# Feed-forward buffers over a whole chunk, the two linear polynomial parts once per chunk, and the first chunk in halves

## The chip, the cores and the metric

The kernel runs on one core of one Trainium2 chip. The metric is the device time of one execution in microseconds (us). Before the change six runs took 249.60 to 254.32 us, with a median of 250.72. The core has five engines that work through their own instruction lists in order and wait for each other by semaphores: TensorE (PE, matmuls), VectorE (DVE), ScalarE (ACT), GpSimd (POOL) and SyncE (SP). Here POOL and SP do little more than start transfers, which the core's 16 DMA engines carry out.

## The reference

The first half is an attention with polynomial features, for 4 batches, 4 heads, 1088 tokens and head width 32. With S1 and S2 of 8 rows each, the features of a row x are the 64 products of S1 x and S2 x. The output of the first half is

```python
kv  = einsum('bhsf,bhsd->bhfd', phi(k), v)
num = einsum('bhsf,bhfd->bhsd', phi(q), kv)
den = einsum('bhsf,bhf->bhs', phi(q), sum(phi(k), over s))[..., None] + 1e-06
x   = (num / den), heads side by side: 4352 tokens x 128
```

The second half is a feed-forward layer with d_ff = 2048 and a rational function between its two matrices:

```python
h = x @ w_in
P = a[0] + a[1]*h + a[2]*h*h + a[3]*h*h*h
Q = 1.0 + abs(b[0])*abs(h) + abs(b[1])*h*h
out = (P / (Q + 1e-06)) @ w_out
```

Inputs and output are float32.

## The kernel before

**Chunks and groups.** Of each batch's 1088 tokens 1024 are two chunks of 512; the 64 left over from each of the four batches form one last chunk of 256. That makes nine chunks, n = 0 to 8. The feed-forward part of a chunk works on tiles with 128 partitions (one block of d_ff) and, along the free axis, blocks times tokens. A group is a set of d_ff blocks: chunks 1 to 7 have two groups of 8 blocks (8 x 512 = 4096 columns), chunk 0 has groups of 4, 4 and 8, the last chunk 8, 4 and 4 blocks of 256 columns. The groups are numbered through, g0 to g19.

**The polynomial.** x is scaled by the ratio of the coefficients (sig) on its way into xT, and a is scaled to match (inv), so that Q is 1 + lsc * (|h| + h*h) up to the small constant. For each group, `add_group` adds these steps: PE makes h in pieces of 1024 columns in PSUM (L572), ACT or DVE evicts each piece to hb in bfloat16 (L184, L186). DVE computes the square s = hb*hb (sq, L582), u = |hb| (ab, L585), the upper linear part t = a3*hb + a2 (hi, L603), t = t*s (cu, L607), and the lower linear part in place, hb = a1*hb + a0 (lo, L610). Two sums follow, u + s (us) and t + hb (ts). Most of them are accumulating transfers that POOL issues (L594), a few run on DVE (L592). ACT takes Ln and then Exp with scale -1 (L614, L618), which gives 1/Q in u. DVE multiplies t by u (ov, L621), and PE projects t with W_out into out_ps (pj, L629). After a chunk's last group out_ps is evicted to oT and stored by SP.

**The attention's steps** are spread between these. For each half batch of keys: transposes (tr), eviction (ev), projection (pr), eviction of a part (ea), products k_p on DVE (pd, L403); then kv. For each chunk of queries: transposes, eviction to qT, two expansions into PSUM (ex0, ex1, L499), eviction of the first to A_sb, their product q_pT on DVE (L506), numerator and denominator on PE in two parts (nd0, nd1, L519), the division in three DVE instructions (dv, L526 to L529), transposes of x (xt, L535) and the scaled eviction to xT (xe, L540 or L542).

**What sets the order.** `plan.add` only collects steps with a name, an engine and their dependencies. ORDER is a list of step numbers written out in full; `Plan.issue` emits the steps in that order, and so fixes the order on each engine. ENGINE names the steps that go to another engine than the default, HOME the PSUM pool of some steps, SKIP the filler matmuls (L746) left out. BUFS gives the number of buffers of each kind. A buffer is taken by the step that names it in `take` and freed when all steps have been emitted that name it in `give`. In the built program an instruction that takes over a buffer waits for the last readers and writers of what lay there: hb, u and t have four buffers and s two, each of one group's 4096 columns.

Of the kernel before, what the change touches and what calls it, by code (L numbers as in the profile page):

```python
# [12 lines left out]
FP = mybir.dt.float32  # L13
# [6 lines left out]
FIRST = [4, 4, 8]  # L20
LAST = [8, 4, 4]
LW = 4096
FILLS = 16

BUFS = dict(xT=3, hb=4, s=2, u=4, t=4, k_sb=2, v=1, q=2, L=1, h_ps=3, out_ps=1, w_ps=1,
            kT=1, a_t=2, k_p=2, qT=2, A_sb=1, q_pT=1, den=1, x=1, oT=1)

ENGINE = {
    "ld.S0": "ACT", "ld.S1": "ACT", "ld.a": "ACT", "ld.b": "ACT", "k00.ea": "DVE", "k01.ea": "DVE", "kr.ev": "DVE",
    "kr.ea": "DVE", "k0.s0": "DVE", "q1.ev": "DVE", "q2.ev": "DVE", "k20.ea": "DVE", "q5.xe": "DVE", "k30.ea": "DVE",  # L30
    "k31.ea": "DVE", "q7.ev": "DVE", "q8.xe": "DVE", "g1.ts": "DVE", "o0.eT": "DVE", "o1.eT": "DVE", "g7.e4": "DVE",
    "o3.eT": "DVE", "o5.eT": "DVE", "g13.e4": "DVE", "g17.us": "DVE", "g18.ts": "DVE", "o8.eT": "DVE",
}

FOUR = []
SKIP = ["f3"]

HOME = {
    "k00.T": "h_ps", "k00.ab": "h_ps", "k01.T": "h_ps", "k01.ab": "h_ps", "kv.0": "h_ps", "q0.T": "h_ps",
    "q0.xT": "h_ps", "q1.T": "h_ps", "k11.T": "h_ps", "q2.T": "h_ps", "q2.xT": "h_ps", "q3.T": "h_ps",  # L40
    "q3.xT": "h_ps", "k20.T": "h_ps", "k21.T": "h_ps", "kv.2": "h_ps", "q4.T": "h_ps", "q5.T": "h_ps",
    "q6.T": "h_ps", "q8.T": "h_ps", "q8.xT": "h_ps", "fill.1": "h_ps", "fill.4": "h_ps", "fill.6": "h_ps",
    "fill.9": "h_ps", "fill.11": "h_ps", "fill.12": "h_ps",
# [3 lines left out]
    27, 4, 26, 30, 0, 36, 1, 31, 6, 56, 20, 3, 32, 33, 37, 5, 41, 38, 39, 57, 23, 46, 29, 2, 42, 40, 58, 43, 47, 59,  # L47
    60, 44, 45, 48, 49, 50, 51, 52, 21, 53, 28, 55, 8, 61, 7, 83, 78, 79, 67, 54, 62, 63, 80, 81, 11, 34, 68, 69, 12,
    64, 65, 84, 22, 9, 66, 82, 70, 71, 72, 85, 86, 215, 216, 35, 217, 10, 87, 218, 230, 232, 231, 233, 24, 245, 16,
    220, 219, 115, 247, 116, 246, 248, 222, 224, 234, 235, 237, 223, 221, 226, 73, 74, 75, 249, 250, 238, 239, 240,  # L50
    76, 25, 251, 93, 94, 236, 77, 252, 253, 254, 227, 266, 268, 270, 88, 89, 267, 269, 256, 257, 241, 242, 95, 97,
    272, 271, 225, 14, 228, 273, 229, 243, 104, 105, 90, 258, 244, 96, 91, 92, 274, 277, 285, 98, 130, 201, 117, 99,
    100, 255, 260, 286, 13, 275, 131, 279, 259, 287, 101, 278, 289, 291, 261, 262, 288, 118, 119, 276, 200, 290, 292,
    102, 103, 120, 121, 263, 293, 294, 296, 297, 281, 306, 106, 307, 108, 122, 123, 325, 326, 280, 107, 109, 124,
    264, 298, 282, 283, 308, 309, 310, 312, 152, 295, 311, 313, 300, 265, 110, 111, 112, 327, 284, 153, 329, 314,
    315, 331, 328, 317, 318, 319, 330, 132, 332, 205, 125, 126, 301, 113, 213, 154, 334, 18, 114, 299, 155, 134, 302,
    333, 127, 128, 129, 316, 133, 346, 303, 336, 135, 338, 17, 156, 348, 321, 337, 304, 347, 349, 189, 350, 320, 190,
    365, 203, 157, 351, 322, 323, 352, 15, 136, 366, 141, 158, 137, 353, 138, 142, 335, 340, 305, 324, 367, 368, 355,
    354, 139, 339, 357, 358, 359, 369, 140, 386, 159, 341, 371, 370, 372, 342, 160, 376, 373, 374, 377, 378, 387, 19,
    143, 145, 356, 361, 360, 343, 388, 389, 344, 161, 390, 392, 391, 393, 144, 167, 362, 168, 146, 405, 395, 375,  # L60
    406, 162, 163, 164, 165, 345, 380, 381, 166, 363, 409, 147, 397, 394, 148, 149, 364, 398, 399, 407, 411, 408,
    379, 382, 150, 151, 410, 412, 414, 416, 413, 418, 169, 171, 396, 383, 178, 401, 426, 427, 428, 429, 170, 417,
    172, 179, 384, 445, 402, 430, 431, 432, 173, 446, 174, 181, 400, 433, 403, 175, 435, 404, 434, 415, 420, 437,
    180, 182, 176, 447, 177, 448, 419, 451, 421, 183, 438, 439, 449, 422, 450, 452, 454, 453, 385, 466, 467, 209,
    436, 441, 468, 469, 423, 485, 486, 424, 456, 457, 184, 185, 186, 440, 442, 470, 471, 458, 487, 472, 204, 488,
    489, 473, 443, 474, 475, 444, 477, 478, 455, 460, 191, 193, 425, 459, 187, 188, 479, 491, 490, 492, 192, 461,
    493, 194, 462, 506, 525, 526, 508, 507, 476, 494, 480, 195, 196, 463, 527, 496, 497, 464, 481, 509, 482, 498,
    495, 510, 511, 512, 513, 528, 465, 529, 483, 197, 514, 198, 515, 517, 519, 499, 500, 484, 530, 531, 214, 532,
    501, 548, 546, 533, 207, 534, 547, 516, 535, 502, 549, 553, 518, 536, 538, 520, 561, 562, 563, 537, 564, 551,
    550, 552, 521, 522, 523, 574, 540, 503, 504, 575, 576, 554, 577, 539, 555, 541, 208, 542, 566, 524, 579, 581,  # L70
    580, 568, 567, 569, 557, 558, 565, 570, 571, 505, 199, 578, 556, 559, 582, 543, 211, 206, 212, 544, 545, 210,
    560, 572, 573, 583, 584, 585, 586, 587, 588, 202,
# [40 lines left out]
def kernel(  # L113
# [27 lines left out]
    GW = GF * CW  # L141
# [14 lines left out]
    SHAPES = dict(xT=([128, CW], FP), hb=([128, GW], BF), s=([128, GW], BF), u=([128, GW], BF), t=([128, GW], BF),  # L156
# [199 lines left out]

    W_by = [big.tile([128, NF // 2, d_model], BF, name=f"w_by{i}") for i in range(4)] if FOUR else []
    by_steps = []
    if FOUR:
        ld["wf"] = load("wf", lambda key: starter(key).dma_start(  # L360
            out=new("L", "wf")[:, :NF // 2 * d_model].rearrange("p (n d) -> p n d", d=d_model),
            in_=moe_w_out.rearrange("(fo fi) d -> fi fo d", fi=128)[:, 0:NF // 2, :]), 1740, pk=1024, take=[("L", "wf")], start="SP")

        def by(i):
            o, s = W_by[i].rearrange("p n d -> p (n d)"), T["L", "wf"][:, :NF // 2 * d_model]
            if ENGINE.get(f"c.w{i}", "ACT") == "ACT":
                nc.scalar.mul(o, s, a_sb[:, i:i + 1])
            else:
                nc.vector.tensor_scalar(out=o, in0=s, scalar1=a_sb[:, i:i + 1], scalar2=None, op0=AX.mult)

        for i in range(4):
            alts = dict(ACT=280 + 0.82 * NF // 2 * d_model, DVE=150 + 0.55 * NF // 2 * d_model)
            by_steps.append(plan.add(f"c.w{i}", ENGINE.get(f"c.w{i}", "ACT"), alts[ENGINE.get(f"c.w{i}", "ACT")], lambda i=i: by(i),
                                     after=[ld["wf"], c_inv], give=[("L", "wf")], alts=alts))

# [104 lines left out]
    def add_queries(n, srcs, nt, owners, loads, kv_steps, give=()):  # L480
# [41 lines left out]
        def divide():  # L522
            nb = min(2, nt)
            nd = pair("nd")[:, :nt // nb, :nb * 132].rearrange("p b (g c) -> p b g c", c=D + 1)
            den = new("den", n)[:, :nt // nb, :nb * H]
            nc.vector.tensor_scalar(out=den, in0=nd[:, :, :, D], scalar1=1e-6, scalar2=None, op0=AX.add)  # L526
            nc.vector.reciprocal(out=den, in_=den)
            x = new("x", n)[:, :nt, :].rearrange("p (b i) (h d) -> p b (i h) d", b=nt // nb, h=H)
            nc.vector.tensor_mul(out=x, in0=nd[:, :, :, 0:D],  # L529
                                 in1=den[:, :, :, None].broadcast_to([128, nt // nb, nb * H, D]))  # L530

        def x_transposes():
            p = new(*ps(nm, "xT"))
            for i in range(nt):
                nc.tensor.transpose(p[:, i * 128:(i + 1) * 128], in_=T["x", n][:, i, :], identity=ident)  # L535

        def x_evac():
            o, i = new("xT", n)[:, :W], T[ps(nm, "xT")][:, :W]
            if ENGINE.get(nm + ".xe", "ACT") == "ACT":
                nc.scalar.mul(o, i, sig)  # L540
            else:
                nc.vector.tensor_scalar(out=o, in0=i, scalar1=sig, scalar2=None, op0=AX.mult)  # L542
# [9 lines left out]
        for i in range(nt // 2):  # L552
            nd.append(plan.add(f"{nm}.nd{i}", "PE", 520, lambda i=i: num_den(i), after=[s] + nd + kv_steps,
                               take=[("h_ps", nm, "nd")] if i == 0 else [], give=[("q_pT", n)]))
        s = plan.add(f"{nm}.dv", "DVE", 560 + 135 * nt, divide, after=nd, take=[("x", n), ("den", n)],
                     give=[("h_ps", nm, "nd"), ("den", n)])
        s = plan.add(nm + ".xt", "PE", 100 * nt + 37, x_transposes, after=[s], take=[ps(nm, "xT")], flex=[ps(nm, "xT")], give=[("x", n)])
        return add_copy(nm + ".xe", x_evac, W, ptr=1, after=[s, c_b], take=[("xT", n)], give=[ps(nm, "xT")])


    def add_group(g, G):
        W, fis, n = G["W"], G["fis"], G["n"]
        gw = W * len(fis)
        nsub = 1024 // W
# [220 lines left out]
```

## Time and profile before

The profiled execution took 249.8 us, of which its span, from the first to the last instruction, is 248.0 us. The table gives the busy time of each engine over the span, and the stages by the time since its start.

| | PE | DVE | ACT | POOL | DMA share | GB/s |
|---|---|---|---|---|---|---|
| whole span, us busy | 221.5 | 225.4 | 213.9 | 48.8 | | 182 |
| 0 to 25 us | 23.06 | 14.05 | 9.69 | 2.69 | 0.76 | 227 |
| 25 to 45 us | 19.87 | 19.80 | 16.33 | 5.55 | 0.84 | 135 |
| 45 to 95 us | 49.02 | 46.70 | 46.21 | 10.06 | 0.97 | 183 |
| 95 to 145 us | 48.80 | 49.12 | 47.94 | 9.10 | 0.99 | 190 |
| 145 to 205 us | 56.94 | 58.67 | 57.19 | 13.08 | 0.98 | 182 |
| 205 to 244 us | 23.46 | 36.63 | 36.53 | 8.36 | 0.98 | 181 |

The DMA share is the mean busy share of the 16 DMA engines. In the slices a digit is the busy share of one fortieth of the span in tenths. In a group's row stand the line, the engine, the operation, the tiles written and read, the shapes and the count; then the busy time in us and the mean of one in ns; then the time that the engine was idle just before, with what ended it. In a timeline row stand the start and the duration in us, and in brackets the idle time before it. An instruction on DVE starts a little before the one ahead of it is recorded as ended.

### The profile page before, as it was taken

The numbers are of one execution on the slowest core, as the hardware profiler recorded it, in microseconds if no ns is written. First come the engines' busy times: TensorE is split into PE (matmuls) and PEld (weight loads), VectorE is DVE, ScalarE is ACT, GpSimd is POOL, SyncE is SP. The second block draws the span as 40 slices with busy tenths as digits, with TensorE's granted clock in tenths as the row PEclk, the third lists the DMA queues.
The fourth block names the chain that finished last, engine by engine and source line by source line (L and its number), as shares of the span: only waits on it lengthen the run. The fifth ranks groups of instructions, "written<-read, shape, count | busy, mean of one in ns | idle before, by whom it ended". The sixth has DMA issues, their size and how long they took to land.

```text
span 248.0 us, 4269 instructions
## 1 busy us (share of the span) xinstructions
PE 221.5 (89%) x1779; PEld 127.2 (51%) x1789; DVE 225.4 (91%) x205; ACT 213.9 (86%) x158; POOL 48.8 (20%) x61
## 2 busy tenths in 40 slices
PE   7999999999999999999999999999998969920763
PEld 2674455654636466563557445546453627720542
DVE  0785999999989989999999999999999999998993
ACT  2336589989989798999999999899989899999991
POOL 4000422132101212112111121212121312113210
PEclk9999999999999999999999999999999999995598
DMA  5895398999998899989999999999999999999982
GB/s 150 266 323 177 69 140 178 168 220 185 186 170 183 146 189 229 231 173 167 173 196 186 180 162 188 196 169 178 200 165 183 178 198 188 182 188 185 196 162 72
DMA packets 23428, 45.11 MB, mean 182 GB/s; under 512 B 5233, under 2 KB 13553, under 8 KB 23409
## 3 DMA queue, kind: packets, MB, share of 16 engines
q0 software_dynamic: 11232, 34.87, 80.0%
q1 hardware_dynamic: 11712, 9.90, 12.8%
q8 instruction: 14, 0.23, 0.4%
q10 hardware_dynamic: 464, 0.08, 0.2%
q14 instruction: 6, 0.04, 0.0%
HBM read 8.79 MB, written 2.23 MB: 44 GB/s over the span
## 4 chain that ended last, share of the span: by engine, by line
PE 37%; DVE 28%; DMA 17%; issue 10%; ACT 6%; SPq 0%; DVEq 0%; ACTq 0%; POOLq 0%
PE h_ps L572 19%; DMA t<-hb 8%; DMA u<-s 7%; DVE s L582 6%; DVE t L621 5%; PE h_ps L499 5%; DVE t L607 5%; PE out_ps L629 4%; DVE t L603 4%; DVE u L585 3%; ACT u L618 3%; DVE hb L610 2%; PE h_ps L421 2%; DMA q<-in_q_dram 2%; PE h_ps L519 2%
## 5 line engine op out<-in xcount | busy, mean ns | idle before, releaser
L572 PE MATMUL h_ps<-xT,w_in_sb 128*128 128x512 f32 (+1 forms) x288 | 125.8, 577 | 3.2 <-ACT hb L184 2.9
L572 PEld LDWEIGHTS h_ps<-xT,w_in_sb 128*128 128x128 f32 x288 | 51.7, 190 | 55.4 <-issue 43.3
L184 ACT CAST hb<-h_ps 128x1024 bf16<-128x1024 f32 x66 | 64.6, 1018 | 8.4 <-PE h_ps L572 8.0
L614 ACT ACTIVATE L<-u,one_ap,lsc 128x4096 f32<-128x4096 bf16 (+2 forms) x20 | 65.9, 3295 | 5.4 <-DMA u<-s 5.0
L618 ACT ACTIVATE u<-L 128x4096 bf16<-128x4096 f32 (+2 forms) x20 | 62.3, 3114 | 0.2
L629 PE MATMUL out_ps<-w_out,t 128*128 128x128 bf16 x544 | 35.2, 225 | 16.0 <-DVE t L621 15.8
L594 POOL DMA_DIRECT2D u<-s x19 | 24.1, 1269 | 118.3 <-DVE u L585 54.7
L629 PEld LDWEIGHTS <-t 128*128 128x128 bf16 x544 | 32.5, 101 | 23.8 <-DVE t L621 20.7
L621 DVE TENSOR_TENSOR t<-t,u 128x4096 bf16<-128x4096 bf16 (+2 forms) x20 | 39.2, 1968 | 3.1 <-DMA t<-hb 1.7
L582 DVE TENSOR_TENSOR s<-hb 128x4096 bf16<-128x4096 bf16 (+2 forms) x20 | 39.2, 1963 | 1.5 <-ACT hb L184 1.5
L607 DVE TENSOR_TENSOR t<-t,s 128x4096 bf16<-128x4096 bf16 (+2 forms) x20 | 39.3, 1967 | 0.3
L594 POOL DMA_DIRECT2D t<-hb x18 | 21.6, 1200 | 72.2 <-ACT u L618 17.4
L610 DVE TENSOR_SCALAR hb<-hb,a_sb 128x4096 bf16<-128x4096 bf16 (+2 forms) x20 | 23.8, 1189 | 0.2
L603 DVE TENSOR_SCALAR t<-hb,a_sb 128x4096 bf16<-128x4096 bf16 (+2 forms) x20 | 23.6, 1183 | 0.0
L585 DVE TENSOR_SCALAR u<-hb 128x4096 int16<-128x4096 int16 (+2 forms) x20 | 22.3, 1115 | 0.1
L499 PE MATMUL h_ps<-qT,Srep 64*128 64x512 f32 (+1 forms) x72 | 19.5, 617 | 0.4 <-ACT hb L184 0.4
L506 DVE TENSOR_TENSOR q_pT<-A_sb,h_ps 128x1024 f32<-128x1024 f32 (+1 forms) x9 | 10.4, 1157 | 2.6 <-ACT A_sb L184 1.4
L519 PEld LDWEIGHTS h_ps<-kv,q_pT 128*64 128x64 f32 (+1 forms) x288 | 8.7, 134 | 5.1 <-issue 2.0
L519 PE MATMUL h_ps<-kv,q_pT 128*64 128x66 f32 (+1 forms) x288 | 10.1, 225 | 0.0
L184 ACT COPY A_sb<-h_ps 128x1024 f32<-128x1024 f32 (+1 forms) x9 | 8.7, 963 | 0.8 <-PE h_ps L499 0.8
L499 PEld LDWEIGHTS h_ps<-qT,Srep 64*128 64x128 f32 x72 | 5.4, 184 | 6.9 <-ACT hb L184 2.1
L184 ACT COPY kT<-h_ps 128x512 f32<-128x512 f32 x5 | 2.9, 585 | 5.4 <-PE h_ps L383 4.8
(89 smaller groups left out, 134.6 us busy)
## 6 DMA issues: line engine op xcount, KB each, us to landing
u<-s POOLq DMA_DIRECT2D x15, 1024.0 KB, 8.7
t<-hb POOLq DMA_DIRECT2D x15, 1024.0 KB, 9.3
k_sb<-in_k_dram SPq DMA_DIRECT2D x4, 512.0 KB, 4.7
q<-in_q_dram SPq DMA_DIRECT2D x8, 256.0 KB, 5.1
v<-in_v_dram SPq DMA_DIRECT2D x4, 512.0 KB, 7.9
out_dram<-oT SPq DMA_DIRECT2D x8, 256.0 KB, 6.5
w_in_sb<-in_moe_w_in_dram SPq DMA_DIRECT2D x2, 512.0 KB, 5.3
u<-s POOLq DMA_DIRECT2D x2, 512.0 KB, 7.5
```

Of the source, the lines that this page charges most:

```text
L184: nc.scalar.copy(out=out, in_=in_)
L499: nc.tensor.matmul(pair(i)[:, g, :W], lhsT=Srep[i][rows].rearrange("p g f -> p (g f)"), rhs=T["qT", n][rows, :W], start=True, stop=True)
L572: nc.tensor.matmul(p[:, i * W:(i + 1) * W], lhsT=w_in_sb[:, fi * 128:(fi + 1) * 128], rhs=T["xT", n][:, :W], start=True, stop=True)
L582: nc.vector.tensor_mul(out=new("s", g)[:, :gw], in0=h, in1=h)
L585: nc.vector.tensor_scalar(out=new("u", g)[:, :gw].bitcast(mybir.dt.int16), in0=T["hb", g][:, :gw].bitcast(mybir.dt.int16), scalar1=0x7FFF, ...
L594: nc.gpsimd.dma_start(out=d, in_=s, accum_op=AX.add, max_dma_last_dim=4096)
L603: nc.vector.tensor_scalar(out=new("t", g)[:, :gw], in0=T["hb", g][:, :gw], scalar1=a_sb[:, 3:4], scalar2=a_sb[:, 2:3], op0=AX.mult, op1=AX ...
L607: nc.vector.tensor_mul(out=T["t", g][:, :gw], in0=T["t", g][:, :gw], in1=T["s", g][:, :gw])
L614: nc.scalar.activation(out=new("L", g, l0)[:, :lw], in_=T["u", g][:, l0:l0 + lw], func=ACT.Ln, bias=one_ap, scale=lsc)
L618: nc.scalar.activation(out=T["u", g][:, l0:l0 + lw], in_=T["L", g, l0][:, :lw], func=ACT.Exp, scale=-1.0)
L621: nc.vector.tensor_mul(out=T["t", g][:, :gw], in0=T["t", g][:, :gw], in1=T["u", g][:, :gw])
L629: nc.tensor.matmul(T["out_ps", n][:, j * 128:(j + 1) * 128], lhsT=T["t", g][:, c:c + 128], rhs=W_out[:, fis[i], :], start=fis[i] == 0 and ...
```

## The change

The groups of a chunk now share buffers of the whole chunk's width: hb, s, u and t have 16 x 512 = 8192 columns, of which hb, u and t have two buffers and s one, so that the space is the same. `add_group` becomes `add_chunk`, which adds all steps of a chunk. For chunks 1 to 7, hi and lo (the names in WIDE) are one instruction each over 8192 columns; all other steps keep their groups as column ranges of the shared tiles. hi waits for all eight evictions of the chunk, and a buffer is freed for a later chunk when all ranges of it are done with.

Chunk 0's groups become 2, 2, 4 and 8 blocks. Its division, the transposes of x and the scaled eviction are done in two halves of 256 tokens, and its first h piece is computed in four matmuls of 256 columns, the first two of them after the first half. Step numbers change, and ORDER, ENGINE, HOME and SKIP are replaced: all engines' orders differ, SP's loads among them (the first half of w_in is issued after q1's load, v_rem, the keys of batch 1 and q_rem, where it stood ahead of v_rem). DVE makes three of the h evictions where it made two, and the sums g0.us, g1.us, g18.us and g19.ts where it made g1.ts, g17.us and g18.ts. The code of FOUR, which was an empty list, is gone. ORDER and HOME are left out here.

```diff
-FIRST = [4, 4, 8]
+FIRST = [2, 2, 4, 8]
 LAST = [8, 4, 4]
 LW = 4096
+WIDE = ["hi", "lo"]
+SPLIT = [0]
-BUFS = dict(xT=3, hb=4, s=2, u=4, t=4, k_sb=2, v=1, q=2, L=1, h_ps=3, out_ps=1, w_ps=1,
+BUFS = dict(xT=3, hb=2, s=1, u=2, t=2, k_sb=2, v=1, q=2, L=1, h_ps=3, out_ps=1, w_ps=1,
             kT=1, a_t=2, k_p=2, qT=2, A_sb=1, q_pT=1, den=1, x=1, oT=1)
-FOUR = []
-SKIP = ["f3"]
+SKIP = ["f6", "f15", "f3", "f2"]
...
-    GW = GF * CW
+    FW = NF * CW
...
-    SHAPES = dict(xT=([128, CW], FP), hb=([128, GW], BF), s=([128, GW], BF), u=([128, GW], BF), t=([128, GW], BF),
+    SHAPES = dict(xT=([128, CW], FP), hb=([128, FW], BF), s=([128, FW], BF), u=([128, FW], BF), t=([128, FW], BF),
...
+        if n in SPLIT:
+            out = []
+            for i in range(2):
+                s = plan.add(f"{nm}.dv{i}", "DVE", 830, lambda i=i: divide(i), after=[nd[i]] + out[-1:], give=[("h_ps", nm, "nd"), ("den", n)],
+                             take=[("x", n), ("den", n)] if i == 0 else [])
+                s = plan.add(f"{nm}.xt{i}", "PE", 240, lambda i=i: x_transposes(i), after=[s], take=[ps(nm, "xT", i)],
+                             flex=[ps(nm, "xT", i)], give=[("x", n)])
+                out.append(add_copy(f"{nm}.xe{i}", lambda i=i: x_evac(i), W // 2, ptr=1, after=[s, c_b] + out[-1:],
+                                    take=[("xT", n)] if i == 0 else [], give=[ps(nm, "xT", i)]))
+            return out
...
-    def add_group(g, G):
+    def add_chunk(n, W, sizes, g0, x_step, prev_o, store):
...
+        whole = [(f"w{n}", 0, NF)]
+
+        def units(op):
+            return whole if op in WIDE and 0 < n < len(chunks) else parts
+
+        def at(buf, f0, f1):
+            return T[buf, n][:, f0 * W:f1 * W]
...
-        def d_low():
-            nc.vector.tensor_scalar(out=T["hb", g][:, :gw], in0=T["hb", g][:, :gw], scalar1=a_sb[:, 1:2],
-                                    scalar2=a_sb[:, 0:1], op0=AX.mult, op1=AX.add)
+        def d_lo(f0, f1):
+            nc.vector.tensor_scalar(out=at("hb", f0, f1), in0=at("hb", f0, f1), scalar1=a_sb[:, 1:2], scalar2=a_sb[:, 0:1],
+                                    op0=AX.mult, op1=AX.add)
...
+                if n in SPLIT and f0 == 0:
+                    hm = plan.add(f"{nm}.i{f0 - a}", "PE", 880, lambda f0=f0: h_mm(f0, 0), after=[x_step[0]] + loads, take=[("h_ps", n, f0)])
+                    hm = plan.add(f"{nm}.h{f0 - a}", "PE", 880, lambda f0=f0: h_mm(f0, 1), after=[x_step[-1], hm] + loads, give=last)
...
+        wide("sq", d_sq, "s", tt, ["e"])
+        wide("ab", d_ab, "u", ts, ["e"])
+        sum_of("us", "u", "s", ["sq", "ab"], [("s", n)])
+        wide("hi", d_hi, "t", tp, ["e", c_inv])
+        wide("cu", d_cu, None, tt, ["hi", "sq"], give=[("s", n)])
+        wide("lo", d_lo, None, tp, ["hi", "ab", "sq"])
+        sum_of("ts", "t", "hb", ["cu", "lo"], [("hb", n)])
```

The new helpers `wide` and `sum_of` add one step per range: `wide` on DVE, over the ranges that `units` returns, with the steps it depends on found by overlapping ranges; `sum_of` over the groups, on POOL or DVE by ENGINE, as before. In the new file ov is L628, the POOL sums L619 and the projection L635.

## The prediction

> **What bounds the kernel now.** I read the slices first, then the instruction groups by shape, then VectorE (DVE) in order of time. Slices and queue share:
>
> ```profile
> PE   7999999999999999999999999999998969920763
> DVE  0785999999989989999999999999999999998993
> ACT  2336589989989798999999999899989899999991
> DMA  5895398999998899989999999999999999999982
> q0 software_dynamic: 11232, 34.87, 80.0%
> ```
>
> From slice 4 (25 us) to 39 DVE is at 9 almost throughout; ACT and the DMA engines come close behind. So a gain must start DVE's stream earlier, shorten it, or take gaps out of it. DVE's rows by shape:
>
> ```profile
> L607 DVE TENSOR_TENSOR t<-t,s 128x4096 bf16<-128x4096 bf16 x15 | 34.3, 2288 | 0.3
> L610 DVE TENSOR_SCALAR hb<-hb,a_sb 128x4096 bf16<-128x4096 bf16 x15 | 20.3, 1351 | 0.1
> L603 DVE TENSOR_SCALAR t<-hb,a_sb 128x4096 bf16<-128x4096 bf16 x15 | 20.2, 1344 | 0.0
> L603 DVE TENSOR_SCALAR t<-hb,a_sb 128x2048 bf16<-128x2048 bf16 x3 | 2.4, 806 | 0.0
> ```
>
> L603 grows by 538 ns from 2048 to 4096 columns, so some 270 ns of each are fixed. The timeline of DVE shows where its feed-forward stream starts and where it ends:
>
> ```profile
> 20.12 1.22 DVE L506 TENSOR_TENSOR q_pT<-A_sb,h_ps 128x1024 f32<-128x1024 f32 x1 [1.41 <-ACT A_sb L184]
> 22.17 1.21 DVE L403 TENSOR_TENSOR k_p<-a_t,w_ps 128x1024 f32<-128x1024 f32 x1
> 24.84 1.23 DVE L582 TENSOR_TENSOR s<-hb 128x2048 bf16<-128x2048 bf16 x1 [1.46 <-ACT hb L184]
> 28.28 1.79 DVE L585 TENSOR_SCALAR u<-hb 128x2048 int16<-128x2048 int16 x1
> ...
> 242.95 0.69 DVE L621 TENSOR_TENSOR t<-t,u 128x1024 bf16<-128x1024 bf16 x1 [0.35 <-DMA t<-hb]
> ```
>
> Starts are closer than durations, since the end of one instruction overlaps the next start. I therefore cost DVE by spacing without a gap: 2.20 us for a two-input op at 4096, 1.13 at 2048, 0.61 at 1024; 1.26, 0.73, 0.45 for L603/L610; 1.13, 0.61, 0.34 for L585; 1.13 for each 1024-column float32 op or h eviction. From 24.84 to 243.64 pass 218.8 us. The instructions there add up to 207.6 at these spacings, so 11.2 are gaps: 6.3 that the timeline names (3.0 before 93 us, 1.6 in the middle, 1.7 in the tail) and 4.9 unnamed, 1.1 of them in the first L585, which lasted 1.79 where another of its size takes 0.69.
>
> [...] The POOL issues of 1 MB last 1.19 to 1.97 us among DVE ops[...].
>
> ```profile
> u<-s POOLq DMA_DIRECT2D x15, 1024.0 KB, 8.7
> t<-hb POOLq DMA_DIRECT2D x15, 1024.0 KB, 9.3
> 147.00 1.39 POOL L594 DMA_DIRECT2D u<-s  x1 [6.03 <-DVE u L585]
> 155.47 3.81 ACT L614 ACTIVATE L<-u,one_ap,lsc 128x4096 f32<-128x4096 bf16 x1 [0.56 <-DMA u<-s]
> ```
>
> The first two are median issue-to-landing; the last two one case: 8.5 us with the previous sum issued 7.2 us earlier. With one 5.3 us earlier (t<-hb issued at 219.49, its L621 at 228.74) it was 9.25. POOL starts 0.3 to 0.4 us after the producer's successor starts on DVE.
>
> **The parts.** *DVE's stream.* One 8192-column hi or lo for two of 4096 in chunks 1 to 7. By the 259 ns per 1024 columns of the spacings an 8192 takes 1.26 + 1.06 = 2.32 against 2.52: 14 × 0.2 = 2.8 saved. Unseen width: if nothing is fixed it saves 0; by durations (1.344 + 1.076 against 2.69) 3.8. I take 2.8. Splitting chunk 0's first 2048-column group into two of 1024 adds 0.09 for each of four two-input ops, 0.17 for hi and lo, 0.07 for abs: 0.8. One more h eviction on DVE (3, not 2) adds 1.1; one more k_p falls into this phase, 1.1; the other copies change by 0. Sum: 207.6 − 2.8 + 0.8 + 1.1 + 1.1 = 207.8. So the wide ops, as spent, buy nothing net. ACT's own total (one h eviction fewer, two short Ln/Exp pieces more) and the bytes of the POOL sums (5120 columns of sums on DVE in both) are equal.
>
> *The start.* In the new program k11's transposes and projection move behind the first h matmuls on PE; k10's and both expansions of q1 still stand ahead of them. Laid out with the trace's durations: k00 transposes at 5.00 as now; k_rem's transposes stand ahead of k00's projection and may wait for k_rem until 7.6 at the latest (when it was used without a wait), costing up to 1; kv complete on PE at 12.6 and its copies on DVE at 14.15 (now 14.76); first numerator half on PE until 14.75, both until 15.3 (now 16.34); the five scalar ops of a_sb and lsc stand on DVE ahead of the first divide, until 15.15, so divide, transpose, scale end at 17.2; the second half's at 19.1, since q1's expansions (1.06 each) and k10's projection (0.6) stand between on PE. The first four quarter-matmuls run 18.6 to 20.35 (now 20.06 to 21.8), ACT evicts until 21.4, and DVE, which does q_pT and k_p (2 × 1.13) from 19.1, starts abs at 21.5. It needs one eviction, where the 2048-column group needs two. That is 3.3 us before 24.84.
>
> On SP, the first w_in load moves behind q1's load, four v_rem, k1 and four q_rem issues. It was issued at 5.97; the issues ahead of it ran until some 12, and with the 5.3 us to landing it arrives at 17.3, needed at 18.6. Cover 1.3.
>
> *Chunk 0 and 1.* Small groups run out of work. The 2048 group's hi waits for the fourth eviction: PE ends it at 27.5, ACT at 28.6, DVE is there at 27.6: 1.0. The 4096 group's square waits for the eighth, at 36.2: 0.6. The third group's last product waits for its Exp behind a transfer of 7.5 and two evictions, 46.0 against 44.2: 1.8. DVE's own eviction in chunk 1 waits for PE: 1.1. Sum 4.5, against 3.0 named now. I count the 1.1 of the L585 as not recurring.
>
> *Middle.* Now a sum t<-hb has some 15 us of DVE work between its issue and its reader L621 (issued 115.59, read at 130.01). After, both halves' sums leave together, late (lo is one op), and DVE has between the issue and the first half's reader: 8.8, 8.4, 8.6, 8.8, 8.8, 8.4, 9.1 us for chunks 1 to 7. Against 0.4 + 8.5, with 9.2 where the sum ahead is closer than 6 us (chunk 5), the waits are 0.1 to 0.8, together 2.0. While DVE waits there, the next chunk's abs and squares queue behind it, and with them the sums that ACT's Ln waits for; they slip by the same amount, counted once. The s buffer is one chunk: the next chunk's first square waits for both sums u<-s, 12.3 to 17 us after the second one's inputs, against 9: cover 3. The first eviction of chunk n waits for both t<-hb of chunk n − 2, landed 13 us or more before DVE needs the group: hidden, though PE and ACT queue behind it. Middle now 1.6, after 2.0.
>
> *Tail.* Same groups (8, 4, 4), same kind of order: 1.7 again; last product to end 4.4 as now.
>
> *Sum.* 21.5 + 207.8 + gaps (4.5 + 2.0 + 1.7 + 3.8 unnamed) 12.0 = 241.3. Span + 4.4 = 245.7; + 1.8 outside the span = 247.5, against 249.8 for the same execution now: 2.3 less. That execution is 0.9 below the median 250.72, so I say 248.4.
>
> **Rivals.** (1) *The start doesn't come.* w_in lands at 19 to 20 (issue as late as the last q_rem now, 13.5), or k_rem is waited for. The matmuls start at 20, DVE at about 23; 1.5 are lost, and the result is 249.9.[...] Against: the cover of 1.3. Chance 0.18.
> (2) *Slower: paired sums land late.* After each chunk two t<-hb leave 2 to 3.5 us apart, then the next u<-s. Now they alternate 4 to 8 us apart. DMA shares are already 0.95 to 1.05 in the stretches of 20 us. If the first of the pair is slowed by the second, to 10.5 (the longest measured is 11.5), each of seven chunks waits 1.9 more: 13 us, 261; at 9.6, 7 us, 255. It decides from 0.35 us per chunk (8.9 landing), where the gain of 2.3 is gone. Against: the tail now has sums 5.2 us apart landing in 9.25 to 9.5. Chance 0.22.
> (3) *More gain.* The merged ops save 3.8 and the waits of chunks 0 and 1 vanish, as the order was laid out around them: 245. Chance 0.10.
> Forecast as worked: 0.50.
>
> **How the numbers follow.** Within 0.5% means 249.5 to 252.0, about what runs of this kernel can tell from no change. Faster: most of the forecast (0.45), rival 3, a little of rival 1: 0.58. Same: the rest of the forecast, most of rival 1, mild cases of 2: 0.19. Slower: 0.23. The range reaches from rival 3 to a mild rival 2, 244.5 to 254.5, which leaves out half of rival 2 and a little below; the forecast alone spans 246.5 to 250.
>
> **What would show it.** First feed-forward op on DVE at 21 to 22; hi and lo at 8192 lasting 2.4; t<-hb landing near 8.5 to 9.3, with first-half L628 waiting under 1 us each; last L628 ended near 241. Wrong if DVE starts at 23 or later, if L628 waits for t<-hb sum to over 5, or if ACT's evictions wait for t<-hb landings and starve the hi ops.

## The result, and the profile after

The changed kernel takes 252.74 us (median of 36 runs, 252.30 to 254.17), the kernel before 251.15 (73 runs on the same chip, 249.56 to 254.40). The ratio is 1.0066, with a 95% interval of 1.0054 to 1.0079: 1.7 us slower, where 2.3 us faster was forecast. Medians here and below are over all runs; the ratios leave out the few runs that lie over 1.5% above the fastest of their kernel. The profiled execution took 252.71 us, 250.9 of them span. That of the kernel before, 249.8, was a quick one, 1.4 below its median, so of the 2.9 us between the two spans only some 1.6 are the kernels' difference.

The slices of the changed kernel and its queue share:

```profile
PE   7999999999999999799999999899979999750871
DVE  1768898979999899799989999999999999999891
ACT  2344888988989979999989989999998999999980
DMA  5975898999779999999969999999999999999980
q0 software_dynamic: 11376, 34.87, 79.1%
```

Counted from slice 0, DVE is fuller in slice 3 (8, it was 5), but emptier in slice 2 (6, it was 8), and has 7s at 8 and 16 and 8s at 6, 13 and 20, where it had 9s. The DMA row has 7s at 10 and 11 and a 6 at 20, where it had 9s. TensorE's row (PE) is 9 from slice 1 to 24 but for one 7. DVE's costliest groups by shape:

```profile
L609 DVE TENSOR_TENSOR t<-t,s 128x4096 bf16<-128x4096 bf16 x15 | 34.2, 2282 | 0.0
...
L605 DVE TENSOR_SCALAR t<-hb,a_sb 128x8192 bf16<-128x8192 bf16 x7 | 17.2, 2463 | 0.2
L612 DVE TENSOR_SCALAR hb<-hb,a_sb 128x8192 bf16<-128x8192 bf16 x7 | 16.9, 2408 | 0.1
```

A wide hi or lo lasts 2.41 to 2.46 us on average against two of 1.34 to 1.35. So one wide hi is 0.23 us shorter than the two it replaces and one wide lo 0.29, where the forecast counted 0.2. The timeline of DVE, at its start and at its longest waits:

```profile
22.87 0.43 DVE L601 TENSOR_SCALAR u<-hb 128x1024 int16<-128x1024 int16 x1
...
30.48 0.81 DVE L605 TENSOR_SCALAR t<-hb,a_sb 128x2048 bf16<-128x2048 bf16 x1 [1.04 <-ACT hb L188]
...
51.90 2.29 DVE L598 TENSOR_TENSOR s<-hb 128x4096 bf16<-128x4096 bf16 x1 [2.00 <-DMA u<-s]
...
104.83 0.17 DVE L515 TENSOR_SCALAR den<-h_ps 128x16 f32<-128x16 f32 x1 [1.44 <-PE h_ps L504]
...
129.31 0.17 DVE L515 TENSOR_SCALAR den<-h_ps 128x16 f32<-128x16 f32 x1 [1.16 <-PE h_ps L504]
...
245.84 0.69 DVE L628 TENSOR_TENSOR t<-t,u 128x1024 bf16<-128x1024 bf16 x1 [1.51 <-DMA t<-hb]
```

and the transfers of 1 MB, median from issue to landing:

```profile
u<-s POOLq DMA_DIRECT2D x15, 1024.0 KB, 10.6
t<-hb POOLq DMA_DIRECT2D x15, 1024.0 KB, 9.0
```

Before, these were 8.7 and 9.3. Against the prediction's sum, in us:

| term | predicted | in the trace |
|---|---|---|
| first feed-forward operation on DVE | 21.5 | 22.87 |
| DVE's work from there, by the same spacings | 207.8 | 207.8 |
| waits in chunks 0 and 1 (30.48, 38.60, 51.90) | 4.5 | 3.8 |
| waits for PE after that (five, the longest 1.44 and 1.16) | 0 | 3.7 |
| first-half products waiting for t<-hb (in the trace without chunk 7's 0.39, which is in the tail) | 2.0 | 1.35 |
| tail | 1.7 | 2.7 |
| unnamed | 3.8 | 4.3 |
| last product ends | 241.3 | 246.53 |
| behind it, and outside the span | 4.4 + 1.8 | 4.4 + 1.8 |

This says where DVE stood idle. The runs below show that it doesn't say why.

### The profile page after: what moved, and what is told of

Read it like the earlier page. It is cut to its first block, busy times and chain, and to the rows that moved or that the text cites. A ratio compares the mean times of both kernels' runs of the same rounds, so it can differ in the third digit from the quotient of the medians.

```text
span 250.9 us, 4268 instructions
## 1 busy us (share of the span) xinstructions
PE 224.8 (90%) x1782; PEld 130.4 (52%) x1787; DVE 224.0 (89%) x203; ACT 214.4 (85%) x159; POOL 52.5 (21%) x62
## 3 DMA queue, kind: packets, MB, share of 16 engines
q0 software_dynamic: 11376, 34.87, 79.1%
## 4 chain that ended last, share of the span: by engine, by line
PE 28%; DMA 26%; DVE 22%; issue 15%; ACT 6%; POOL 1%; DVEq 0%; POOLq 0%; ACTq 0%
PE h_ps L589 14%; DMA u<-s 12%; DMA t<-hb 11%; DVE s L598 4%; DVE t L605 4%; DVE t L628 4%; PE h_ps L484 4%; ACT L L622 3%; DVE u L601 3%; PE h_ps L504 3%; DVE t L609 3%; PE out_ps L635 2%; DMA k_sb<-in_k_dram 2%; DVE q_pT L491 1%; ACT u L625 1%
## 5 line engine op out<-in xcount | busy, mean ns | idle before, releaser
L589 PE MATMUL h_ps<-xT,w_in_sb 128*128 128x512 f32 (+1 forms) x292 | 125.0, 570 | 1.3 <-ACT hb L188 0.7
L589 PEld LDWEIGHTS h_ps<-xT,w_in_sb 128*128 128x128 f32 x292 | 52.7, 190 | 54.2 <-issue 44.8
L188 ACT CAST hb<-h_ps 128x1024 bf16<-128x1024 f32 x65 | 63.8, 1016 | 11.0 <-PE h_ps L589 10.5
L635 PE MATMUL out_ps<-w_out,t 128*128 128x128 bf16 x544 | 37.5, 231 | 15.4 <-DVE t L628 15.3
L635 PEld LDWEIGHTS <-t 128*128 128x128 bf16 x544 | 34.2, 104 | 24.4 <-DVE t L628 20.7
L619 POOL DMA_DIRECT2D t<-hb x20 | 23.9, 1197 | 97.6 <-DVE t L609 55.2
L619 POOL DMA_DIRECT2D u<-s x18 | 25.0, 1390 | 90.8 <-DVE u L601 30.1
L628 DVE TENSOR_TENSOR t<-t,u 128x4096 bf16<-128x4096 bf16 (+2 forms) x21 | 39.5, 1880 | 4.2 <-DMA t<-hb 4.0
L605 DVE TENSOR_SCALAR t<-hb,a_sb 128x8192 bf16<-128x8192 bf16 (+3 forms) x14 | 22.4, 1598 | 1.3 <-ACT hb L188 1.0
L612 DVE TENSOR_SCALAR hb<-hb,a_sb 128x8192 bf16<-128x8192 bf16 (+3 forms) x14 | 22.0, 1572 | 0.3
L601 DVE TENSOR_SCALAR u<-hb 128x4096 int16<-128x4096 int16 (+2 forms) x21 | 21.2, 1018 | 0.0
## 6 DMA issues: line engine op xcount, KB each, us to landing
u<-s POOLq DMA_DIRECT2D x15, 1024.0 KB, 10.6
```

The source lines that it names most:

```text
L188: nc.scalar.copy(out=out, in_=in_)
L589: nc.tensor.matmul(p[:, i * W + c0:i * W + c1], lhsT=w_in_sb[:, fi * 128:(fi + 1) * 128], rhs=T["xT", n][:, c0:c1], start=True, stop=True)
L601: nc.vector.tensor_scalar(out=at("u", f0, f1).bitcast(mybir.dt.int16), in0=at("hb", f0, f1).bitcast(mybir.dt.int16), scalar1=0x7FFF, scala ...
L605: nc.vector.tensor_scalar(out=at("t", f0, f1), in0=at("hb", f0, f1), scalar1=a_sb[:, 3:4], scalar2=a_sb[:, 2:3], op0=AX.mult, op1=AX.add)
L619: nc.gpsimd.dma_start(out=at(dst, f0, f1), in_=at(src, f0, f1), accum_op=AX.add, max_dma_last_dim=4096)
L628: nc.vector.tensor_mul(out=at("t", f0, f1), in0=at("t", f0, f1), in1=at("u", f0, f1))
```

## The experiments

Every ratio is to runs of the kernel before on the same chip; the changed kernel stands at 1.0066.

| run | base and edit | median us | ratio, 95% interval |
|---|---|---|---|
| e1 | changed; wide ops given as two | 252.65 | 1.0068, 1.0043 to 1.0094 |
| e2 | changed; squares in half-chunk buffers | 252.47 | 1.0064, 1.0042 to 1.0087 |
| e3 | changed; last group earlier on DVE | 252.73 | 1.0074, 1.0048 to 1.0101 |
| e4 | changed; remainder keys behind k01 on PE | 253.96 | 1.0140, 1.0097 to 1.0183 |
| e5 | changed; first product in bf16, loads converted | 255.69 | 1.0192, 1.0164 to 1.0219 |
| e6 | before; the same | 254.62 | 1.0158, 1.0126 to 1.0189 |
| e7 | before; hi and lo each in two | 253.48 | 1.0109, 1.0072 to 1.0145 |
| e8 | before's order with chunk-wide hb, u, t | 250.56 | 0.9967, 0.9938 to 0.9997 |
| e9 | changed; half the columns of each POOL sum | 247.27 | 0.9838, 0.9795 to 0.9881 |
| e10 | before; the same | 247.66 | 0.9859, 0.9816 to 0.9902 |
| e11 | changed; two sums on DVE | 255.32 | 1.0163, 1.0122 to 1.0204 |
| e12 | changed; chunks by halves | 280.93 | 1.1188, 1.1130 to 1.1245 |
| e13 | changed; first product from upper halves | 249.55 | 0.9925, 0.9897 to 0.9954 |
| e14 | before; the same | 250.73 | 0.9984, 0.9954 to 1.0014 |
| e15 | e13 with half sums | 243.43 | 0.9695, 0.9648 to 0.9742 |
| e16 | e14 with half sums | 245.38 | 0.9776, 0.9724 to 0.9827 |
| e17 | e12 with half-chunk squares | 264.27 | 1.0545, 1.0487 to 1.0602 |
| e18 | changed; first product of chunk 0 alone from upper halves | 249.59 | 0.9932, 0.9902 to 0.9961 |

**The named waits, one by one (e1 to e4).** The first theory was that each wait of the trace costs its length, and that the wide operations save theirs.

```diff
-                    fn(f0, f1)
+                    half = f0 + GF if op in WIDE and f1 - f0 > GF else f1
+                    fn(f0, half)
+                    if half < f1:
+                        fn(half, f1)
```

> The changed kernel with each chunk-wide hi and lo of chunks 1 to 7 given as two instructions of 4096 columns, one right after the other, at the same place. If the wide instruction saves the fixed part that the forecast counted (14 x 0.2 us), this run is 2.8 us slower than the changed kernel, 255.5, and its spacings show 1.26 us per instruction. If the wide instruction gives that back elsewhere[...], the run is at 252.7 or below, and POOL's issues of up to 2.97 us are back under 2.

DVE was 2.4 us busier (226.4 against 224.0), and the time did not move. Its waits for t<-hb fell from 4.0 to 2.9 us and those of `den` for PE from 3.0 to 1.7: the added work stands where DVE would have waited. So the 2.8 us that the wide operations save are worth nothing here that the interval (0.6 us to either side) can tell.

```diff
-BUFS = dict(xT=3, hb=2, s=1, ...
+BUFS = dict(xT=3, hb=2, s=2, ...
-    SHAPES = dict(... s=([128, FW], BF), ...
+    SHAPES = dict(... s=([128, FW // 2], BF), ...
```

> The changed kernel with the squares in two half-chunk buffers, the same bytes, released one by one. If the 2.0 us that VectorE waited at 51.9 for the sum u<-s of chunk 0 cost the kernel its full length, that wait is gone, everything after stands 2.0 us earlier, and the time is 250.7. If the transfers are the bound there and only queue up behind each other, the wait comes back at a later sum and the time is 252.2 to 252.7.

The wait at 51.90 is gone, and two others stand in its place. DVE's timeline in this run:

```profile
49.82 2.29 DVE L606 TENSOR_TENSOR s<-hb 128x4096 bf16<-128x4096 bf16 x1
53.00 1.22 DVE L191 CAST hb<-h_ps 128x1024 bf16<-128x1024 f32 x1 [0.90 <-PE h_ps L597]
...
58.43 1.22 DVE L492 TENSOR_TENSOR q_pT<-A_sb,h_ps 128x1024 f32<-128x1024 f32 x1 [0.55 <-PE h_ps L485]
```

The square comes 2.08 us earlier, the next one (g5.sq) only 0.35 (62.23 against 62.58). The second branch of the expectation said that transfers would take the gain; in these lines both waits are for TensorE. This was the first sign of the cause.

```diff
+MOVES = [("g20.hi", "g17.ov"), ("g20.lo", "g17.ov"), ("g20.cu", "g17.ov")]   # ahead of
```

> The changed kernel with hi, lo and cubic product of the last group (1024 columns) ahead of the last product of chunk 7's second half on VectorE, so that the last sum t<-hb leaves 3.5 us earlier. If the tail's waits were made by the order, the wait of 1.51 us before the last product falls away up to the last Exp (ended 244.7): last product ends at 245.2 where it was 246.45, time 251.5. If the landing is set by the transfers ahead on the queue, the sum leaves earlier and lands no earlier: 252.7.

The sum left at 237.11 instead of 240.91 and was no longer waited for. But chunk 7's last product, which stands behind the moved steps, frees out_ps through its projection, and DVE waited for that:

```profile
242.55 0.69 DVE L202 COPY oT<-out_ps 128x512 f32<-128x512 f32 x1 [2.94 <-PE out_ps L647]
```

One wait of 2.94 for one of 1.51 and one of 0.78. Neither expectation had it.

```diff
+MOVES = [("kr.tr", "k00.ea"), ("kr.ev", "k01.ea"), ("kr.pr", "k0.rem"), ("kr.ea", "k0.rem"), ("kr.pd", "k0.rem")]
-    "sT": "h_ps", "k00.T": "h_ps",
+    "kr.ab": "h_ps", "sT": "h_ps", "k00.T": "h_ps",
```

> The changed kernel with the remainder keys' transposes and projection moved back behind k01's on TensorE, as in the kernel before. If they held up k01's projection (at 9.93, before at 9.06) and with it the sums kv, the first feed-forward operation starts at 22.1 to 22.4 (22.87 now) and the time is 252.0 to 252.2. If the start is set by what stands between kv and the first matmuls, or chunk 0's evictions bound what follows, the start moves by under 0.2 and the time stays at 252.7.

It went the other way. k01's projection did come earlier (8.90, not 9.93), but the remainder's now stood behind kv's first matmuls (12.62), and kv's copies on DVE, which need both, started at 15.86, not 14.92. The first h matmul moved from 19.90 to 20.83, the first feed-forward operation from 22.87 to 23.81, and the time grew by 1.2 (by the ratios 1.9). Here a delay of TensorE and VectorE together passes to the end; 2.4 us of VectorE's work alone didn't.

**VectorE and the buffers in the kernel before (e7, e8).**

> The kernel before with each hi and lo of 4096 columns given as two instructions of 2048 (1.46 us by the spacings against 1.26): 30 x 0.2 = 6 us more work on VectorE. If VectorE bounds the kernel before, as the prediction took it, the time is 256 to 257. If TensorE does, VectorE has slack and takes most of it in: below 254.

DVE was 5.9 us busier (231.3 against 225.4), and the time grew by 2.7 (1.8 to 3.6 by the interval). So about half of added work on VectorE reaches the end of the kernel before: VectorE counts there, but is not the only bound.

e8 runs the new code with the old groups, order, ENGINE and HOME, `WIDE = []`, `SPLIT = []`, hb, u and t a chunk wide.

> The kernel before, its own order and its own operations by group, with one buffer per chunk for hb, u and t (released only when both groups are done) and half-chunk buffers for s as they were; five steps of the last two chunks stand elsewhere so that the buffers suffice. If the later release costs the changed kernel its time, this one is at 252.7 or more. If the loss comes from the new order and the chunk-wide operations, it stays within 0.7 us of the kernel before.

It is no slower (the interval ends at 0.9997), with u<-s landing in 8.5 us and t<-hb in 9.4. The later release of the buffers, which the prediction followed buffer by buffer, costs nothing in the old order.

**The transfers (e9 to e11).**

```diff
+                f1 = (f0 + f1) // 2
                 nc.gpsimd.dma_start(out=at(dst, f0, f1), in_=at(src, f0, f1), accum_op=AX.add, max_dma_last_dim=4096)
```

> The changed kernel, in which every sum made by a transfer adds only the first half of its columns (the other half of the sums is left out): half the bytes of u<-s and t<-hb, everything else as it was. If the transfers bound the kernel (their engines were busy 0.98 to 1.04 in nearly every stretch after 75 us), VectorE's waits for them and ACT's are gone and the time falls to VectorE's own: 22.9 start + 207.8 work + 6 of other waits + 6.2 behind it = 243, within 2 us. If transfers only fill what is free, it stays above 250.

> The kernel before with the same edit, half the columns of every sum made by a transfer left out. If the transfers bound both, this one falls to 24.8 + 207.6 + 6 + 6.2 = 244.6, and stands above the changed kernel with the edit: the forecast's order of the two, which the transfers turned round. If the changed kernel's loss doesn't come from transfers, it is still 1.6 us slower than this run.

Both gain, the changed kernel 2.3%, the one before 1.4%, and they end 0.2% apart, which is within the intervals. So transfers hold both, and the changed one more. But neither reaches VectorE's own time. In e9's slices the transfers are no longer full, TensorE and VectorE are:

```profile
PE   7999999999999999999999999899989889690772
DVE  0768898989999999999979999999999999999992
...
DMA  5976595464629437465245444634454464746250
```

```diff
-    "g18.us": "DVE", "g19.ts": "DVE", "o8.eT": "DVE",
+    "g18.us": "DVE", "g19.ts": "DVE", "o8.eT": "DVE", "g9.ts": "DVE", "g13.ts": "DVE",
```

> The changed kernel with two of its sums t<-hb of 1 MB (second half of chunks 3 and 5) made on VectorE instead: 2 x 2.2 us more work there, 2 MB less for the transfers, which take 5 to 6 us per MB where they follow each other. If the transfers bound the kernel, it gains more than the work costs: 250 to 251.7. If VectorE bounds it, 4.4 more: 257.

By the ratios this took 2.4 us more than the changed kernel, for 4.4 of work. The 5 to 6 us per MB agree with the changed kernel's queue share: 34.87 MB in 79.1% of 250.9 us are 5.7 us per MB. The DMA share between 125 and 150 us fell to 0.67 from 0.93, to no use. Transfers don't bind alone either.

**By halves (e12, e17).** `WIDE = []`, and in ORDER for each of chunks 1 to 7:

```diff
-w3.hi g7.ov g8.cu w3.lo g8.ts g9.cu g9.ts
+g8.hi g8.lo g8.cu g8.ts g7.ov g9.hi g9.lo g9.cu g9.ts
```

> The changed kernel with hi and lo by halves in chunks 1 to 7, and all three operations of the first half (hi, lo, cubic product) together at the place of the wide hi, those of the second half together at its cubic product, so that the first half's sum t<-hb leaves 3 to 5 us earlier and not together with the second's. VectorE's work grows by 14 x 0.2 = 2.8 us. If the chunk-wide lo, which holds back both sums, left the transfers without work (their share fell to 0.6 around 128 us), the loss is undone: 250.7 to 251.3. If not, the time is 252.7 or, where VectorE bounds, up to 255.5.

The run says nothing on its question. POOL issues chunk 1's sums in turn: u<-s at 54.62, t<-hb at 60.96 and the second u<-s only at 68.59 (65.16 in the changed kernel, where t<-hb follows at 72.92). So the second u<-s of a chunk now stands behind the first t<-hb, and the single s buffer makes the next chunk's square wait for it. The waits of DVE in this run:

```profile
DVE s L612 <- DMA u<-s: 19.4, 5, 7.2
```

The single s buffer and sums in turn don't go together; in the changed kernel both u<-s of a chunk leave before its t<-hb.

> The changed kernel with hi and lo by halves as in the run before with that name, the sums in turn (u<-s, t<-hb of the first half, then of the second), and half-chunk buffers for the squares; VectorE's two evictions of a chunk's last pair stand behind the first half's cubic product, which no longer needs them. VectorE's work is 2.8 us more than in the changed kernel. If the chunk-wide operations made TensorE and the transfers bind, the time falls below the kernel before: 249.5 to 251. If the new order of everything else did, it stays at 252.5 to 254.

With s by halves these waits are gone. At chunk 3's second product the run is 1.9 us ahead of the changed kernel (147.59 against 149.45); later q_pT on DVE waits 6.0 us for PE, which waits for an eviction on DVE (3.1), and the time is 264. This order follows one rule for all chunks and isn't tuned, so whether the chunk-wide operations are what makes the transfers weigh more stays open.

**TensorE (e5, e6, e13 to e16, e18).** The changed kernel's TensorE in order of time, where chunk 0's first products are made in eight pieces of 1024 columns (counted as x4 in a row of 128x512 float32):

```profile
19.90 1.89 PE L589 MATMUL h_ps<-xT,w_in_sb 128*128 128x256 f32 x8
21.63 0.60 PE L368 MATMUL h_ps<-ident,k_sb 128*128 128x128 f32 x4
22.06 1.88 PE L589 MATMUL h_ps<-xT,w_in_sb 128*128 128x512 f32 x4
23.88 0.69 PE L504 MATMUL h_ps<-kv,q_pT 128*64 128x66 f32 x16
24.50 0.66 PE L472 MATMUL h_ps<-ident,q 128*128 128x128 f32 x4
25.08 0.69 PE L377 MATMUL w_ps<-S,kT 128*64 128x64 f32 x16
25.70 3.70 PE L589 MATMUL h_ps<-xT,w_in_sb 128*128 128x512 f32 x8
...
33.92 3.60 PE L589 MATMUL h_ps<-xT,w_in_sb 128*128 128x512 f32 x8
```

and that of the kernel before:

```profile
20.06 8.85 PE L572 MATMUL h_ps<-xT,w_in_sb 128*128 128x512 f32 x20
...
34.69 1.88 PE L572 MATMUL h_ps<-xT,w_in_sb 128*128 128x512 f32 x4
```

The kernel before makes five pieces in a run and has all eight at 36.6. The changed kernel starts 0.16 earlier and works without a gap, but has four pieces by 29.4 (the kernel before by 27.1) and all eight at 37.5. q1's numerators and transposes of x stand between the pieces in both kernels. New there are k11's transposes and projection (21.63 and 25.08) and q2's transposes (24.50), which the kernel before makes ahead of the pieces and behind them; it has k20's transposes between them instead (28.75). VectorE started 2.0 us earlier on a supply that ends 0.9 later. To test what TensorE's load is worth, it was taken away.

```diff
-    SHAPES = dict(xT=([128, CW], FP), ...
+    SHAPES = dict(xT=([128, CW], BF), ...
-    w_in_sb = big.tile([d_model, d_ff], FP, name="w_in_sb")
+    w_in_sb = big.tile([d_model, d_ff], BF, name="w_in_sb")
-    ld["wi"] = [load(f"wi{i}", lambda key, i=i: starter(key).dma_start(
+    ld["wi"] = [load(f"wi{i}", lambda key, i=i: nc.gpsimd.dma_start(
```

> The changed kernel with the feed-forward's first product computed from bf16 copies of its two inputs, instead of float32: w_in is converted to bf16 as it is loaded (its two loads leave from POOL, not SP), xT is written in bf16. It leaves out float32 precision there[...]. If TensorE sets the pace from 20 to 208 us (it stood idle for under 6 us in it), this kernel is bound by VectorE again: start 22.9, 207.8 of work, some 10 of waits, time 246 to 248. If the transfers of the sums set it, the time stays at 252 to 252.7.

> The kernel before with the same edit (the feed-forward's first product from bf16 copies, w_in converted as it is loaded). If TensorE sets the pace of both kernels, this one gains too, to 247 to 249, and the changed kernel with the edit is then no slower than this one: the forecast's gain of VectorE shows once TensorE doesn't hide it. If the changed kernel's loss comes from its own waits (buffers, transfers), it remains 1.5 us or more slower than this run.

Both became slower, since the edit also moved their start: with the converting loads in flight k_rem landed late, in e5 TensorE waited 2.85 us for it (0.23 in the changed kernel), and the first feed-forward operation came at 27.49. By the medians the changed kernel made up 1.7 of these 4.6 us by its end (2.5 in its profiled execution, the fastest of five), the one before next to nothing of its 3.6. The next four runs read the upper halves of the float32 values instead, so that the loads stay.

```diff
-                nc.tensor.matmul(... lhsT=w_in_sb[:, fi * 128:(fi + 1) * 128],
+                nc.tensor.matmul(... lhsT=w_in_sb.bitcast(BF)[:, fi * 256 + 1:(fi + 1) * 256:2],
```

> The changed kernel with the feed-forward's first product from bf16: xT written in bf16, and of each float32 of w_in only the upper 16 bits read as bf16 (the lower half left out), so that no load changes. The start is as in the changed kernel (22.9), unlike in the run whose loads were converted. If TensorE and transfers both hold the kernel back, this one gains a little, 250 to 251.5; if TensorE alone, 246 to 248; if it is not held by TensorE at all, 252.7.

> The kernel before with the same edit (upper halves of w_in, xT in bf16). The run with converted loads started 3.6 us late and ended 3.65 us late, so TensorE held nothing in it: 250.5 to 251.3. If TensorE does bound it, 247 to 249.

The kernel before stays where it is, the changed kernel goes from 0.7% slower than the unedited kernel before to 0.75% faster. So the load of these matmuls holds back the changed kernel, and the one before by 0.5% at most. In e14 VectorE's stream starts 1.6 us earlier than before the edit, and chunk 0's eighth piece ends at 34.6, 2.0 earlier:

```profile
23.25 1.22 DVE L582 TENSOR_TENSOR s<-hb 128x2048 bf16<-128x2048 bf16 x1
```

This lead doesn't reach the end. TensorE itself waits 5.9 us there for VectorE's division of q1. In both runs the granted clock fell (to 0.844 from 0.965 and to 0.834 from 0.969), and in e13 the matmuls of the expansions, which the edit left as they were, took longer (722 ns on average, 629 in the changed kernel), which takes back part of what the edit saves.

> The changed kernel with both taken away: bf16 first product (upper halves of w_in) and half the columns of every sum made by a transfer left out. VectorE and ACT remain. By the prediction's own sum without its waits for transfers: 22.9 + 207.8 + 2 to 5 of other waits + 6.2 = 239 to 242. If VectorE's sum was wrong, it stays at 246 to 247.

> The kernel before with both taken away: 24.8 + 207.6 + 3 to 6 + 6.2 = 242 to 245, and 2 to 3 us above the changed kernel with the same edits, if the forecast's gain is there once TensorE and the transfers don't hide it. If the two are within 0.7 us, the gain never was on VectorE.

By the ratios the two are 2 us apart in the forecast's direction (by the medians 1.5, without the one run of e16 at 250.03), but the intervals overlap at their ends (0.9742 and 0.9724), and the two profiled spans stand the other way (243.5 and 241.7). That the forecast's gain is on VectorE, with TensorE and transfers both out of the way, isn't settled by them.

In e13 most of the gain was there early: the second product t<-t,u started 2.20 us sooner than in the changed kernel, the last but one 2.58. Hence chunk 0 alone:

```diff
+                w, x = w_in_sb[:, fi * 128:(fi + 1) * 128], T["xT", n][:, c0:c1]
+                if n == 0:
+                    w, x = (z.bitcast(BF)[:, 1::2] for z in (w, x))
+                nc.tensor.matmul(p[:, i * W + c0:i * W + c1], lhsT=w, rhs=x, start=True, stop=True)
```

> The changed kernel with the first product of chunk 0 alone (32 of 292 matmuls and their quarter pieces) from the upper 16 bits of w_in and xT read as bf16, the lower halves left out. If the lead of VectorE's earlier start is lost to TensorE's work in chunk 0, the first four products t<-t,u come as early as with all chunks shortened (44.7 where the changed kernel has 46.9) and most of the lead lasts: 249.8 to 251. If TensorE, without a gap until 100 us, takes it back in chunks 1 to 3, the time is 252 to 252.7.

| start of the product t<-t,u, in us | 1st | 2nd | 4th | 9th | 16th |
|---|---|---|---|---|---|
| changed kernel | 36.02 | 46.93 | 75.94 | 135.81 | 220.01 |
| e13, all chunks shortened | 34.82 | 44.73 | 73.73 | 132.45 | 217.43 |
| e18, chunk 0 shortened | 34.89 | 44.81 | 72.96 | 131.95 | 216.94 |

Chunk 0 alone gives all of it, 3.1 us by the medians against the changed kernel, and makes a kernel that is faster than both (0.9932 of the one before), at the price of bf16 inputs to chunk 0's first product. The last two pieces of chunk 0 on PE, which the changed kernel has from 33.92 to 37.52:

```profile
32.29 2.00 PE L592 MATMUL h_ps<-xT,w_in_sb 128*128 128x512 bf16 x4
```

DVE's timeline there shows no wait until the square at 48.90, which in the changed kernel started at 51.90:

```profile
22.88 0.42 DVE L603 TENSOR_SCALAR u<-hb 128x1024 int16<-128x1024 int16 x1
...
29.36 0.81 DVE L607 TENSOR_SCALAR t<-hb,a_sb 128x2048 bf16<-128x2048 bf16 x1
...
36.63 2.28 DVE L600 TENSOR_TENSOR s<-hb 128x4096 bf16<-128x4096 bf16 x1
...
48.90 2.29 DVE L600 TENSOR_TENSOR s<-hb 128x4096 bf16<-128x4096 bf16 x1 [1.07 <-DMA u<-s]
```

The start is the same 22.88; what changed is that TensorE now waits for the evictions (3.3 us in all, the longest 2.00) and no longer the other way round. Later waits shrink with it, in chunks whose matmuls were left as they were: those of `den` for PE at 104.83 and 129.31 from 1.44 and 1.16 to 0.55 and 0.22, while those for t<-hb grow from 4.0 to 4.9 in all.

So TensorE was through with chunk 0 3.2 us earlier, and 3.1 of them reached the end: this is shown for the changed kernel. Two things are not. e18 took away more than the change had put in (the eighth piece is 2.3 us ahead of the kernel before, not level with it), and no run put the steps of k11 and q2 back to their old places; that their place makes the loss is inferred from the PE timelines. And why a lead in chunk 0 lasts in the changed kernel and, by e14, not in the one before, stays open.

## Why the prediction was wrong

**The step that failed is the first one:** "So a gain must start DVE's stream earlier, shorten it, or take gaps out of it." It took VectorE's 9s as the bound of both kernels and passed over the row above them, in which TensorE has 9s from slice 1 to 29. In the window from 25 to 50 us TensorE is busy for 25.00 of 25.00 us after, and was for 24.87 before. Behind chunk 1 its sum has no term for TensorE: VectorE's waits for PE there were put at nothing and came to 3.7 us. With a start 1.4 us later than laid out, a tail 1.0 longer and 0.5 more unnamed, less 1.35 by which the other waits were shorter, that is the 5.2 us by which the last product came late. For the kernel before the step was half right: by e7 VectorE was in part its bound, by e14 TensorE held it by 0.5% at most. For the changed kernel it was wrong.

Term by term:

**The start.** Counted as 3.3 us that last to the end. Measured: 1.97 at the first operation, since kv's copies on DVE ended at 15.40 (laid out for 14.15), the first divide started at 16.63 and the quarter matmuls at 19.90 (18.6), on a TensorE with no gap over 0.23 us. Even the 1.97 was no gain: the prediction noted that k11's steps "move behind the first h matmuls on PE", and booked only what that takes away ahead of them. It did not book them where they went, between chunk 0's pieces. The eighth piece came 0.9 us later than before, and by e18 time on that supply passes to the end. The waits at 30.48 and 38.60 were forecast as 1.0 and 0.6 and measured 1.04 and 0.76; they were the sign of the supply, and were read as small gaps of small groups.

**The wide operations.** Their size was right (2.41 to 2.46 us), and the sum had already spent it. e1 shows more: on this kernel it has no value that can be told from noise. VectorE's work of 207.8 came out as forecast.

**The s buffer.** The "cover 3" was worked out from chunks 1 to 7. At the seam of chunks 0 and 1 the second sum is issued at 42.33, its reader is reached at 49.9, and the cover of 7.6 is short of the 9.45 that it took: 2.0, not counted. It hardly matters: e2 removes it and gains 0.35 at the next square, since the wait for PE at DVE's eviction, forecast as 1.1, then comes out at 0.90.

**The rest.** The waits for t<-hb in the middle were 1.35, not 2.0. Rival 2, sums in pairs landing at 9.6 to 10.5, did not come for t<-hb (9.0), but for u<-s (10.6, once 12.15 from 82.09): that Ln started 1.84 late, three evictions stood behind its Exp, PE waited 1.37 for their PSUM buffers, and `den` 1.44 at 104.83. The tail was 2.7 and not 1.7; e3 shows that its order has no slack to take this out simply. Rival 1, the start that doesn't come, had the right start (DVE at about 23) by luck, for the wrong reason: w_in was not waited for, and k_rem for 0.23 us. None of the three signs of being wrong that the prediction named came true (DVE started at 22.87, L628 waited 4.0 for t<-hb, and no eviction on ACT waited for a transfer): all three looked at VectorE and the transfers.

**Open:** how much of the loss the place of k11's and q2's steps makes; why a lead in chunk 0 lasts in one kernel and not in the other; why halving the transfers' bytes gives the changed kernel 2.3% and the one before 1.4%.

## What to carry to other kernels

Where three engines and the transfers all show 9s, the waits of one of them are not a list of costs: here adding 2.4 us of work on VectorE, or removing a wait of 2.0, moved nothing. A step moved out of the way on a full engine has to be booked where it lands. Before adding up gaps, ask for each busy engine what the kernel does if its load is halved in one stage; here the shortening of one chunk's matmuls told more than the removal of any named wait. A lead at the start is no gain in itself: here the engine that feeds the stream had to lead too (e18), and in the kernel before not even that was enough (e14).

## What the runs showed of the hardware

- A float32 piece took 1.77 us in a run of five (8.85, in the kernel before); two bf16 pieces read from every second 16-bit value took 1.08 in e18 (at 24.25), 0.54 each: a factor of 3.3, with the strided reading in it. All first products together kept TensorE busy for 125.0 us in the changed kernel and for 44.3 in e13, at a lower clock.
- With all first products shortened (e13) TensorE's mean granted clock fell to 0.844 from 0.965. In the windows of 25 us from 25 to 225 it was 0.71 to 0.93, with TensorE busy for 14.5 to 18.4 us of each; the changed kernel's windows with 25.00 busy (25 to 50, 75 to 100, 125 to 150) have 1.00. The matmuls of the expansions, which the edit left as they were, lasted 722 ns on average in e13, 629 in the changed kernel and 614 in e18. Shortening chunk 0 alone left the mean clock at 0.961, but in e18 two pieces took 1.08 us at 24.25 and 2.00 at 32.29, behind waits of TensorE of 2.00 and 1.94; in the slice from 31.0 to 37.2 us the granted clock has a 7, and 9s in all others up to 216 us.
- Next to the 8192-column operations three POOL issues (at 142.85, 189.86 and 213.41) lasted 2.34, 2.97 and 2.34 us; with two of 4096 in their place the same three took 1.28, 1.90 and 1.28 in e1. The runs don't show why; the kernel's time was the same in both (ratios 1.0066 and 1.0068).
- Sums of one size landed after different times. Sums of 512 KB took 4.6 to 4.8 us (medians) in e9 and e10, where all were halved. In the kernel before, two u<-s of 512 KB issued at 26.99 and 31.49 landed after 5.7 and 9.3; the DMA share was 0.32 from 20 to 30 us and 1.17 from 30 to 40. Two of 1 MB issued 2.2 us apart in the changed kernel (126.49 and 128.69) landed after 8.0 and 11.7 us.
